# Two heads in one kernel (a long convolution and linear attention): constants in another order, head masks made late, the ones column carried by x, due times per stage

## The chip, the cores and the metric

The kernel runs on one core of a Trainium2 chip. The core has five engines, each with its own queue of instructions that it takes in order: PE (TensorE, matrix products into PSUM), DVE (VectorE), ACT (ScalarE), POOL (GpSimd) and SP (SyncE, which here only issues DMAs). They run side by side and wait for each other through semaphores. The metric is the device time of one execution in microseconds (us). PSUM has eight banks of 128 x 512 float32; PE can't write a bank until its last reader is done with it.

## The reference

The output is 2048 x 1152 in bfloat16: the left 576 columns come from part A, the right 576 from part B.

```python
# A: k shifted over four taps, times v, a convolution over the sequence, times q
k_shift = sum over t of k_pad[:, t:t + S, :] * shift_k[:, ks - 1 - t]
kv = k_shift * v
y = irfft(rfft(kv, 2S) * rfft(ssm_k, 2S))[:S] + kv * ssm_D
a = q * y
# B: linear attention with 32 heads of 18 features
q, k, v = split(x @ wqkv)
phi = lambda t: where(t > 0, t + 1, exp(t)) + 1e-6
kv  = phi(k)^T v   (per head);   z = sum over s of phi(k)
o   = (phi(q) kv) / (phi(q) z + 1e-6)
b   = o @ wo
```

S is 2048 and D is 576 in both.

## The kernel before

Both parts run interleaved, so that one has work for an engine where the other waits. Nothing of the order is written out by hand: each step is given to a planner (`_Sched`) as an operation with a due time (`key`), an assumed duration for each engine that could do it, the operations it depends on and the buffers it uses. `plan()` then plays the program through: of all operations that could go it takes the one that could start first, ties by due time. Evictions of PSUM may go to ACT or DVE (`evac`, `copy`, L337 to L343); the planner takes the engine on which they would end first, with `PEN` added for DVE. Evictions are made due `EVK` earlier. The planned order becomes the program order of each engine; on the chip only semaphores set the times.

**Constants** (`_consts_fft`, L76 to L137; `_consts_b`; `_consts_heads`, L42 to L73) are made ahead of the planned program. The Fourier matrices Gre and Gim (128 x 16 x 128) are sines of integers that DVE works out (L92 to L97) from iotas of POOL; the small matrix Wsm is a sine too (L136). ACT needs another function table for sines than for exponentials and loads it with a separate instruction. `_consts_heads` makes the masks that cut the products of heads out of larger products (maskbd with fourteen selects of 18 columns, L47 and L49), selectors and ones. They are read by the stages kv, z, bc of part B.

**Part B.** x is loaded in four DMAs (L369), transposed on PE in eight groups (L387) and copied to xT (L341 or L339). Its last tile holds features 448 to 575 in rows 0 to 127, of which row 0 is overwritten with ones by a memset on POOL (L394), and the weights have a row of ones at the same place (L324), which adds one to each product. K is 16 row blocks in two halves of 288 columns, each of five matmuls (L408); ACT takes the exponential (phi_k, L411), DVE makes phi (pk, L414). G is x^T phi(k) (L438), with a column of ones behind x and behind pk (L420, L421) that gives the sums; then the small stages kv, z, M; then four groups of q (L552, L555, L560), denominators (L572 to L585), their transposes and spreading to features (L605), the products (L611), and the output product (L629), evicted to ob and stored (L635).

**Part A** runs in five chunks of channels, four of 128 and one of 64 (`chunk`, from L685). For each: load of the filter (h_sb, L697), transposing load of k (kT, L700), loads of v and q for pairs of chunks (L670), the diagonal matrices of the taps (dg, L709, on DVE), transposes of the filter (hT, L721), a first Fourier step s1 (L739, evicted to Ch or Cu), a transpose of 32 x 32 blocks on DVE (L755), a second step s2 with Wsm (L770, evicted to Th or Tu), a copy X of Th with rows exchanged by DMA (L791), the taps (cv, L806) and u = taps times v (L813). Then the products of the spectra (L825), the way back: is1 (L841), its eviction V, a transpose Vt (L853), is2 (L866, L867), the product with q (L873) and the store (L878).

All DMAs go through SP's queue. Dc and swT (L647 to L653) are tiny loads of ssm_D and shift_k; Ere and Eim are Gre and Gim transposed by DMA. The due times of part A are linear in the stage: `k0(t)` is the start of the chunk plus t times one factor.

Of the kernel before, what the change touches and what calls it, by code (L numbers as in the profile page):

```python
# [20 lines left out]
FX = [0, 128, 256, 384, 448]  # L21
# [7 lines left out]
EVK, HK = 2.75, 1.0  # L29
TB0, TBS = 8.0, 1.44  # L30
TA0, TAP = 12.0, 24.83
# [10 lines left out]
def _consts_heads(nc, cpool, K):  # L42
    maskbd = cpool.tile([128, 126], FP32, name="maskbd")
    nc.gpsimd.memset(maskbd[:], 1.0)
    for hh in range(7):
        blk = maskbd[:, hh * 18:(hh + 1) * 18]
        nc.gpsimd.affine_select(out=blk, in_=blk, compare_op=ALU.is_ge, fill=0.0, base=-18 * hh,  # L47
                                pattern=[[0, 18]], channel_multiplier=1)
        nc.gpsimd.affine_select(out=blk, in_=blk, compare_op=ALU.is_ge, fill=0.0, base=18 * hh + 17,  # L49
                                pattern=[[0, 18]], channel_multiplier=-1)  # L50
# [25 lines left out]
def _consts_fft(nc, cpool, cw, K):  # L76
# [29 lines left out]
    def field(name, shift, mask):  # L106
        t = tmp.tile([128, 1], I32, name=name + "_i")
        if shift:
            nc.vector.tensor_single_scalar(out=t[:], in_=pidx[:], scalar=shift, op=ALU.logical_shift_right)
        nc.vector.tensor_single_scalar(out=t[:], in_=t[:] if shift else pidx[:], scalar=mask, op=ALU.bitwise_and)  # L110
        f = tmp.tile([128, 1], FP32, name=name)
        nc.vector.tensor_copy(out=f[:], in_=t[:])
        return f
    lo4, b4 = field("lo4", 0, 15), field("b4", 4, 1)
    hi4, b0 = field("hi4", 1, 15), field("b0", 0, 1)
# [6 lines left out]
    for w, (row, ri, coef, ipat, base, opat) in enumerate(spec):  # L122
# [5 lines left out]
        if ri is not None:  # L128
            oc = tmp.tile([128, 1], FP32, name="oc%d" % w)
            nc.vector.tensor_scalar(out=oc[:], in0=ri[:], scalar1=coef, scalar2=None, op0=ALU.mult)  # L130
            nc.vector.tensor_scalar(out=off[:, w, :], in0=off[:, w, :], scalar1=oc[:, 0:1], scalar2=None, op0=ALU.add)
        nc.vector.scalar_tensor_tensor(out=wi[:, w, :], in0=idx[:, w, :], scalar=row[:, 0:1], in1=off[:, w, :],
# [16 lines left out]
class _Op:  # L149
    def __init__(self, key, eng, fn, deps, bufs, dma):  # L150

        if any(x.cls == 'PS' for x in bufs) and 'PE' not in eng:
            key -= EVK
# [3 lines left out]
        self.start = self.end = None  # L157
        for b in bufs:
            b.users.append(self)


class _Sched:
# [3 lines left out]
    PEN = 0.23  # L166
# [8 lines left out]
    def op(self, key, eng, fn, deps=(), bufs=(), dma=0.0):  # L175
        o = _Op(key, eng, fn, list(deps), list(bufs), dma)
        self.ops.append(o)
        return o
# [21 lines left out]
    def plan(self):  # L200
        left = list(self.ops)
        order = []
        while left:
            best = None
            for o in left:
                if any(d.end is None for d in o.deps):
                    continue
                ready, taken, ok = 0.0, {}, True
# [23 lines left out]
                rank = (round(st, 2), o.key)  # L232
                if best is None or rank < best[0]:
                    best = (rank, fin, e, st, o, taken)
            if best is None:
                raise RuntimeError("no operation can go: %s" % [o.key for o in left[:8]])
# [11 lines left out]
            left.remove(o)  # L248
            order.append(o)
        order.sort(key=lambda o: o.start)  # L250
# [12 lines left out]
def kernel(  # L263
# [30 lines left out]
                 {'PE': 6.0, 'ACT': 9.5, 'DVE': 9.0, 'POOL': 8.0, 'SP': 0.8})  # L294
# [14 lines left out]
    K = {}  # L309
    cwork = [work.tile([128, 4096], BF, name="cw%d" % i, tag="W8_%d" % i) for i in range(2)]  # L310
    _consts_fft(nc, cpool, cwork, K)
# [5 lines left out]
    nc.gpsimd.memset(neg1[:], -1.0)  # L317
    Ere = cpool.tile([128, 16, 128], BF, name="Ere")
    Eim = cpool.tile([128, 16, 128], BF, name="Eim")
    xT = cpool.tile([128, 5, S], BF, name="xT")  # L320
    wk = cpool.tile([128, 5, D], BF, name="w_k")
    for w in (wk,):
        nc.gpsimd.memset(w[0:64, 4, :], 0.0)
        nc.gpsimd.memset(w[0:1, 4, :], 1.0)  # L324
    _consts_heads(nc, cpool, K)
# [8 lines left out]
    for t in rb:  # L334
        nc.gpsimd.memset(t[:], 0.0)
# [9 lines left out]
    def evac(n):  # L345
        return {'ACT': 0.2 + n * 0.0008, 'DVE': 0.07 + n * 0.00104}
# [6 lines left out]
    tB = [TB0]  # L353

    def kb(cost):
        tB[0] += cost * TBS
        return tB[0] - cost * TBS

    xb = _Buf('X18', 'x_sb')
    pb = _Buf('X18', 'pk')  # L360

    def xview(b):
        return b.t.rearrange("p (r f) -> p r f", f=D + 1)

    xv = x.rearrange("(r p) f -> p r f", p=128)
    d_x, o_xT = [], []

    def load_x(g):
        d_x.append(dma(0.1 if g == 0 else 1.5 + 0.1 * g, 0.59, lambda g=g: nc.sync.dma_start(  # L369
            out=xview(xb)[:, 4 * g:4 * g + 4, 0:D], in_=xv[:, 4 * g:4 * g + 4, :]), (), (xb,)))  # L370

    load_x(0)
    d_w = [dma(1.0, 0.59, lambda: nc.sync.dma_start(
        out=wk[:, 0:4, :], in_=wqkv[0:512, D:2 * D].rearrange("(t p) n -> p t n", p=128)))]
    d_w.append(dma(1.1, 0.08, lambda: nc.sync.dma_start(out=wk[64:128, 4, :], in_=wqkv[512:576, D:2 * D])))
    for g in range(1, 4):
        load_x(g)

    for g in range(8):
        key = TB0 + g * 2.4 * TBS - 1.5  # L380
        ps = _Buf('PS', 'xT_ps', 2)

        def mm(e, g=g, ps=ps):
            pv = ps.t.bitcast(BF)[:, 0:1280].rearrange("p (t s) -> p t s", t=5)
            for rr in range(2):
                for t in range(5):
                    nc.tensor.transpose(out=pv[:, t, 128 * rr:128 * (rr + 1)],  # L387
                                        in_=xview(xb)[:, 2 * g + rr, FX[t]:FX[t] + 128], identity=ident[:])
        o1 = op(key, {'PE': 0.58}, mm, [d_x[g // 2]], (ps, xb))

        def f(e, g=g, ps=ps):
            copy(e, xT[:, :, 256 * g:256 * (g + 1)],
                 ps.t.bitcast(BF)[:, 0:1280].rearrange("p (t s) -> p t s", t=5))
            nc.gpsimd.memset(xT[0:1, 4, 256 * g:256 * (g + 1)], 1.0)  # L394
# [521 lines left out]
```

## Time and profile before

| | |
|---|---|
| median of 3 runs | 200.14 us (199.23 to 200.71) |
| the profiled execution | 199.92 us |
| its span (first to last instruction) | 198.2 us |
| PE busy | 171.6 us, 87% |
| DVE busy | 174.9 us, 88% |
| ACT busy | 126.5 us, 64% |
| POOL busy | 15.8 us, 8% |
| DMA traffic | 25.81 MB |
| mean granted clock of PE | 0.971 |

A group of the profile gives line, engine, operation, output and inputs by the program's names, how often it ran, its busy time, the mean time of one, and the idle time of its engine just before it with the engine that ended it. A line of the order of time gives start and length, then the same names; a bracket at its end is idle time of that engine before it. A row of stretches gives for each engine the busy time within these microseconds. In the line of slices each digit is a fortieth of the span, in tenths.

### The profile page before, as it was taken

The page shows a single profiled execution, that of the slowest core. Times are in us where ns is not written, and L with a number is a line of the kernel's source. Part 1 is how long each engine was busy: PE and PEld are TensorE (multiplying, and loading weights), DVE is VectorE, ACT ScalarE, POOL GpSimd, SP SyncE. Part 2 cuts the span into 40 slices and gives each one's busy share as a digit, 9 for nine tenths or more (in the row PEclk, how much of TensorE's full clock was granted, in tenths as well). Part 3 has the DMA queues.
Part 4 walks back from the last instruction along what each step waited for, and adds up shares of the span by engine and source line. Part 5 has one row for each costly group of instructions (what it writes and reads, how often), then busy time and mean ns, then how long its engine had stood idle before and what let it go on. Part 6 is the DMA issues. An engine that isn't in the chain of part 4 may idle for free. (4 is left out here: it accounts for less than half of the span.)

```text
span 198.2 us, 5391 instructions
## 1 busy us (share of the span) xinstructions
PE 171.6 (87%) x2277; PEld 130.2 (66%) x2277; DVE 174.9 (88%) x259; ACT 126.5 (64%) x176; POOL 15.8 (8%) x60
## 2 busy tenths in 40 slices
PE   0449999989999999999999999799986999869660
PEld 0426888977688788778577677676765786427450
DVE  7943588999997997899999899999999999999880
ACT  3566878289576755775558978337982749760440
POOL 8970100001000000010000000000000000000000
PEclk9999999999999999999999999999999999985995
DMA  5999999321293049029703934150410130212733
GB/s 188 351 327 227 184 215 313 85 107 47 80 254 82 0 167 256 7 58 312 117 0 113 310 59 146 55 139 0 88 60 33 72 143 13 80 49 90 208 123 55
DMA packets 43548, 25.81 MB, mean 130 GB/s; under 512 B 23044, under 2 KB 41732, under 8 KB 43524
## 3 DMA queue, kind: packets, MB, share of 16 engines
q1 hardware_dynamic: 43524, 25.47, 47.8%
q8 instruction: 17, 0.28, 0.6%
q14 instruction: 7, 0.06, 0.1%
HBM read 12.36 MB, written 4.72 MB: 86 GB/s over the span
## 5 line engine op out<-in xcount | busy, mean ns | idle before, releaser
L408 PE MATMUL ps_all<-w_k,xT 128*128 128x288 bf16 x160 | 24.4, 313 | 4.6 <-DVE xT L341 2.2
L552 PE MATMUL ps_all<-xT,w_k 128*126 128x512 bf16 (+1 forms) x100 | 24.2, 381 | 1.8 <-DVE late_q L611 1.6
L629 PE MATMUL ps_all<-late_w,late_q 126*128 126x288 bf16 (+1 forms) x160 | 23.0, 288 | 1.6 <-DVE late_q L611 1.6
L408 PEld LDWEIGHTS <-xT 128*128 128x128 bf16 x160 | 16.5, 106 | 10.9 <-POOL xT L394 2.6
L806 PEld LDWEIGHTS <-kT 128*128 128x128 bf16 x320 | 21.0, 151 | 2.3 <-issue 1.6
L438 PE MATMUL ps_all<-pk,x_sb 128*128 128x288 bf16 (+1 forms) x160 | 22.2, 287 | 0.0
L806 PE MATMUL ps_all<-dg,kT 128*128 128x128 bf16 (+1 forms) x320 | 21.6, 226 | 0.7 <-DVE Tu L341 0.5
L555 ACT ACTIVATE phi_q<-ps_all,neg_133 126x512 bf16<-126x512 f32 (+1 forms) x20 | 13.6, 687 | 12.8 <-PE ps_all L552 9.2
L414 DVE SCALAR_TENSOR_TENSOR pk<-phi_k,ps_all 128x288 bf16<-128x288 bf16 x32 | 13.5, 449 | 8.1 <-ACT phi_k L411 7.9
L339 ACT ACTIVATE Th<-ps_all 128x1024 bf16<-128x1024 f32 x14 | 13.8, 1021 | 9.2 <-PE ps_all L770 9.1
L411 ACT ACTIVATE phi_k<-ps_all,neg_133 128x288 bf16<-128x288 f32 x32 | 15.5, 501 | 5.8 <-PE ps_all L408 4.4
L629 PEld LDWEIGHTS <-late_q 126*128 126x128 bf16 (+1 forms) x160 | 14.8, 98 | 6.7 <-DVE late_q L611 1.9
L339 ACT ACTIVATE Tu<-ps_all 128x1024 bf16<-128x1024 f32 x11 | 11.0, 1022 | 11.3 <-PE ps_all L770 11.2
L853 DVE STREAM_TRANSPOSE Vt<-V 128x1024 f32<-128x1024 f32 x9 | 18.0, 1995 | 0.2
L438 PEld LDWEIGHTS <-x_sb 128*128 128x128 bf16 x160 | 14.8, 98 | 4.8 <-issue 1.4
L552 PEld LDWEIGHTS <-w_k 128*126 128x126 bf16 (+1 forms) x100 | 12.3, 131 | 8.6 <-issue 2.2
L339 ACT ACTIVATE ob<-ps_all 128x288 bf16<-128x288 f32 x29 | 11.4, 410 | 8.6 <-PE ps_all L629 8.4
L339 ACT ACTIVATE Ch<-ps_all 128x1024 bf16<-128x1024 f32 (+1 forms) x15 | 14.4, 988 | 2.6 <-PE ps_all L739 2.6
L339 ACT ACTIVATE Cu<-ps_all 128x1024 bf16<-128x1024 f32 (+1 forms) x16 | 14.5, 950 | 1.0 <-PE ps_all L739 0.8
L339 ACT ACTIVATE V<-ps_all 128x1024 bf16<-128x1024 f32 x14 | 13.8, 1021 | 1.8 <-PE ps_all L841 1.7
L611 DVE SCALAR_TENSOR_TENSOR late_q<-late_q,ps_all 126x512 bf16<-126x512 bf16 (+1 forms) x20 | 12.4, 679 | 0.6 <-PE ps_all L605 0.6
L560 DVE SCALAR_TENSOR_TENSOR late_q<-phi_q,ps_all 126x512 bf16<-126x512 bf16 (+1 forms) x20 | 12.9, 669 | 0.0
(129 smaller groups left out, 316.0 us busy)
## 6 DMA issues: line engine op xcount, KB each, us to landing
X<-Th SPq DMA_DIRECT2D x18, 256.0 KB, 2.3
h_sb<-in_A_ssm_k_dram SPq DMA_DIRECT2D x5, 512.0 KB, 5.4
x_sb<-in_B_x_dram SPq DMA_DIRECT2D x4, 576.0 KB, 5.0
out_dram<-ob SPq DMA_DIRECT2D x16, 144.0 KB, 1.7
v_p<-in_A_v_dram SPq DMA_DIRECT2D x2, 1024.0 KB, 9.3
q_p<-in_A_q_dram SPq DMA_DIRECT2D x2, 1024.0 KB, 6.5
out_dram<-q_p SPq DMA_DIRECT2D x2, 1024.0 KB
w_k<-in_B_wqkv_dram SPq DMA_DIRECT2D x2, 576.0 KB, 4.4
```

Source lines behind the costliest of these rows:

```text
L339: nc.scalar.activation(out=out_ap, in_=in_ap, func=ACT.Copy, scale=scale)
L408: nc.tensor.matmul(ps.t[:, 0:n1 - n0], lhsT=xT[:, t, r * 128:(r + 1) * 128], rhs=wk[:, t, n0:n1], start=(t == 0), stop=(t == 4))
L411: o2 = op(key, {'ACT': 0.46}, lambda e, ps=ps, eb=eb: nc.scalar.activation(out=eb.t[:, 0:288], in_=ps.t[:, 0:288], func=ACT.Exp, bias=neg1 ...
L414: nc.vector.scalar_tensor_tensor(out=xview(pb)[:, r, n0:n1], in0=eb.t[:, 0:288], scalar=1.0, in1=ps.t[:, 0:288], op0=ALU.min, op1=ALU.max),
L438: nc.tensor.matmul(ps.t[:, 0:n1 - n0], lhsT=xview(xb)[:, r, f0:f0 + 128], rhs=xview(pb)[:, r, n0:n1], start=(r == 0), stop=(r == 15))
L552: nc.tensor.matmul(ps.t[0:hn, 512 * j:512 * (j + 1)], lhsT=wq[:, t, h0:h0 + hn], rhs=xT[:, t, 512 * g:512 * (g + 1)], start=(t == 0), stop ...
L555: o2 = op(key, {'ACT': 0.2 + 0.4 * n}, lambda e, ps=ps, eb=eb, hn=hn, n=n: nc.scalar.activation(out=eb.t[0:hn, 0:512 * n], in_=ps.t[0:hn, ...
L560: nc.vector.scalar_tensor_tensor(out=pqT(g)[0:hn, c:c + n, :], in0=eb.t[0:hn, 0:512 * n].rearrange("p (c n) -> p c n", n=512), scalar=1.0, ...
L611: nc.vector.scalar_tensor_tensor(out=o, in0=o, scalar=EPS, in1=ps.t[0:hn, 0:512 * n].rearrange("p (c n) -> p c n", n=512), op0=ALU.add, op ...
L629: nc.tensor.matmul(ps.t[:, 0:288], lhsT=pqT(g)[0:hn, c, rr * 128:(rr + 1) * 128], rhs=wview(2)[0:hn, c, n0:n1], start=(c == 0), stop=(c == 4))
L806: nc.tensor.matmul(pv[:, bi, 0:dc], lhsT=kTb.t[:, c0:c0 + 16 * 127 + 1:16], rhs=dg[:, j, 0:dc], start=(j == 0), stop=(j == 3))
L853: nc.vector.transpose(out=vt[:, 32 * c:32 * (c + 1), :], in_=V.t[:, 2048 * c:2048 * (c + 1)].bitcast(FP32).rearrange("p (w r) -> p w r", r ...
```

## The change

It does the following:

- The ones column of x is written once by DVE, before x is loaded, and the last tile of xT takes columns 449 to 576 of x instead of 448 to 575, so that row 127 is the column of ones. The weights have their row of ones at 127; the memsets of xT are gone. Two memsets of w_k stand ahead of all other constants on POOL.
- The head masks and two zeroed tiles become one planned operation on POOL (`o_late`), on which the stages that read them depend; maskbd is made by two selects instead of fourteen.
- dg is made by POOL instead of DVE.
- The small fields of the index arithmetic are made by five operations instead of ten; the reciprocal writes bfloat16 itself.
- x's first quarter is loaded in two halves, with the weights between them.
- The assumed durations, the start of each engine, `PEN`, `EVK` and all due times are other numbers; each stage of a chunk has its own due time, and each part of B its own pace.
- The planner's search is written with counters, and ties go by the number of the operation.

In the built program PE has as many matmuls as before. Other instructions change engine by the plan. DVE has 2 more evictions of xT, 1 of V, 3 of ob, 1 of late_q, and fewer of Tu (7 to 2), Cu (4 to 2), Ch (5 to 3), hT, Th, GT (5 to 3), late_w; ACT has the counterparts, and four loads of its function table instead of two. In SP's queue the first chunk's h_sb stands behind x, the weights and the four tiny loads; kT's loads stand between the two pairs of X.

```diff
-FX = [0, 128, 256, 384, 448]
-EVK, HK = 2.75, 1.0
-TB0, TBS = 8.0, 1.44
-TA0, TAP = 12.0, 24.83
+P_B0 = 8.00
...
+P_T0 = 19.57
+P_T1 = 37.72
+P_T2 = 63.63
+P_T3 = 84.60
+P_T4 = 111.14
+P_SC = 0.81
+P_h = -15.98
+P_k = -15.51
...
+P_x = -16.80
+P_cv = 10.00
...
+P_p0 = 26.46
+P_p1 = 55.86
...
+P_EVK = 2.69
+P_PEN = 0.43
...
-    maskbd = cpool.tile([128, 126], FP32, name="maskbd")
+    maskbd = cpool.tile([128, 7, 18], FP32, name="maskbd")
     nc.gpsimd.memset(maskbd[:], 1.0)
-    for hh in range(7):
-        blk = maskbd[:, hh * 18:(hh + 1) * 18]
-        nc.gpsimd.affine_select(out=blk, in_=blk, compare_op=ALU.is_ge, fill=0.0, base=-18 * hh,
-                                pattern=[[0, 18]], channel_multiplier=1)
...
+    nc.gpsimd.affine_select(out=maskbd[:], in_=maskbd[:], compare_op=ALU.is_ge, fill=0.0, base=0,
+                            pattern=[[-18, 7], [0, 18]], channel_multiplier=1)
+    nc.gpsimd.affine_select(out=maskbd[:], in_=maskbd[:], compare_op=ALU.is_ge, fill=0.0, base=17,
+                            pattern=[[18, 7], [0, 18]], channel_multiplier=-1)
...
+    for i, (shift, mask) in enumerate(((0, 15), (4, 1), (1, 15), (0, 1))):
+        nc.vector.tensor_scalar(out=fi[:, i:i + 1], in0=pidx[:], scalar1=shift, scalar2=mask,
+                                op0=ALU.logical_shift_right, op1=ALU.bitwise_and)
+    nc.vector.tensor_copy(out=ff[:], in_=fi[:])
...
-                rank = (round(st, 2), o.key)
+                rank = (round(st, 2), o.key, o.num)
...
-                 {'PE': 6.0, 'ACT': 9.5, 'DVE': 9.0, 'POOL': 8.0, 'SP': 0.8})
+                 {'PE': 5.0, 'ACT': 10.3, 'DVE': 8.5, 'POOL': 6.5, 'SP': 1.2})
...
+    nc.vector.memset(xview(xb)[:, :, D:D + 1], 1.0)
     cwork = [work.tile([128, 4096], BF, name="cw%d" % i, tag="W8_%d" % i) for i in range(2)]
+    wk = cpool.tile([128, 5, D], BF, name="w_k")
+    nc.gpsimd.memset(wk[96:128, 4, :], 1.0)
+    nc.gpsimd.memset(wk[0:64, 4, :], 0.0)
     _consts_fft(nc, cpool, cwork, K)
...
+    nc.gpsimd.memset(xview(pb)[:, :, D:D + 1], 1.0)
...
-    for w in (wk,):
-        nc.gpsimd.memset(w[0:64, 4, :], 0.0)
-        nc.gpsimd.memset(w[0:1, 4, :], 1.0)
-    _consts_heads(nc, cpool, K)
...
+    def late_consts(e):
+        _consts_heads(nc, cpool, K)
+        for t in rb:
+            nc.gpsimd.memset(t[:], 0.0)
+    o_late = op(12.0, {'POOL': 7.0}, late_consts)
...
-        return {'ACT': 0.2 + n * 0.0008, 'DVE': 0.07 + n * 0.00104}
+        return {'ACT': 0.2 + n * 0.0008, 'DVE': 0.14 + n * 0.00105}
...
-    def kb(cost):
-        tB[0] += cost * TBS
-        return tB[0] - cost * TBS
+    def kb(cost, pace):
+        tB[0] += cost * pace
+        return tB[0] - cost * pace
...
+    load_x(0.1, 0, 2)
+    d_w = [dma(0.2, 0.08, lambda: nc.sync.dma_start(out=wk[63:127, 4, :], in_=wqkv[512:576, D:2 * D]), rate=340.0),
+           dma(0.3, 0.59, lambda: nc.sync.dma_start(
+               out=wk[:, 0:4, :], in_=wqkv[0:512, D:2 * D].rearrange("(t p) n -> p t n", p=128)), rate=340.0)]
+    load_x(0.4, 2, 4)
     for g in range(1, 4):
-        load_x(g)
+        load_x(1.5 + 0.1 * g, 4 * g, 4 * g + 4)
...
-                                        in_=xview(xb)[:, 2 * g + rr, FX[t]:FX[t] + 128], identity=ident[:])
+                                        in_=xview(xb)[:, 2 * g + rr, FT[t]:FT[t] + 128], identity=ident[:])
...
-            nc.gpsimd.memset(xT[0:1, 4, 256 * g:256 * (g + 1)], 1.0)
...
-    o_kv = op(key, {'DVE': 1.0}, f, [o1], (ps,))
+    o_kv = op(key, {'DVE': 1.3}, f, [o1, o_late], (ps,))
...
-            nc.vector.reciprocal(out=rden, in_=den)
-            nc.vector.tensor_copy(out=rb[g % 2][:, :, 0:32], in_=rden.rearrange("p (r h) -> p r h", h=32))
+            with nc.allow_low_precision(reason="operand of TensorE"):
+                nc.vector.reciprocal(out=rb[g % 2][:, :, 0:32], in_=den.rearrange("p (r h) -> p r h", h=32))
...
-        T = TA0 + sum(ACH[c][1] for c in ORDER[:n]) / 128.0 * TAP
-        k0 = lambda t: T + t * f * TAP / 30.0 * 1.01
+        T = (P_T0, P_T1, P_T2, P_T3, P_T4)[n]
+        k0 = lambda t: T + t * f * P_SC
...
-                nc.vector.tensor_scalar(out=dg[:, j, 0:dc], in0=ident[:, lo:lo + dc],
+                nc.gpsimd.tensor_scalar(out=dg[:, j, 0:dc], in0=ident[:, lo:lo + dc],
                                         scalar1=swf[:, ci, j:j + 1], scalar2=None, op0=ALU.mult)
-        o_dg = op(k0(-5), {'DVE': 0.5}, fn, [o_sw, g1.get('cv')], (dgb,))
+        o_dg = op(k0(P_dg), {'POOL': 1.3}, fn, [o_sw, g1.get('cv')], (dgb,))
```

## The prediction

> **What bounds the kernel now.** I read the page's busy shares and slices first, then the order of time at the start, then a table of stretches at the end, then the groups by shape.
>
> ```profile
> PE 171.6 (87%) x2277; PEld 130.2 (66%) x2277; DVE 174.9 (88%) x259; ACT 126.5 (64%) x176; POOL 15.8 (8%) x60
> PE   0449999989999999999999999799986999869660
> DVE  7943588999997997899999899999999999999880
> ```
>
> PE and DVE are both near full from slice 4 to slice 36; ACT has a third of the span free and POOL nearly all of it. So two things cost time: what keeps PE from starting, and where DVE is so full that PE waits for it. The start:
>
> ```profile
> 9.94 0.81 DVE L341 COPY xT<-ps_all 128x1280 bf16<-128x1280 bf16 x1
> 10.81 1.14 PE L408 MATMUL ps_all<-w_k,xT 128*128 128x288 bf16 x4 [2.20 <-DVE xT L341]
> 13.50 0.17 POOL L420 MEMSET x_sb<- 128x16 bf16 x1 [0.46 <-DMA x_sb<-in_B_x_dram]
> 13.60 0.60 POOL L394 MEMSET xT<- 1x256 bf16 x2
> 14.00 6.64 PE L408 MATMUL ps_all<-w_k,xT 128*128 128x288 bf16 x31 [2.05 <-POOL xT L394]
> 22.77 5.68 PE L408 MATMUL ps_all<-w_k,xT 128*128 128x288 bf16 x45
> ```
>
> Four of the five matmuls of the first K group run at 10.81; the fifth needs the row of ones in xT's last tile. That memset stands in POOL's queue behind the head masks and behind the ones columns of x, which wait for x to land. K runs only from 14.00. Its first 31 matmuls take 6.64/31 = 0.214 us each, later ones 5.68/45 = 0.126. The end:
>
> ```profile
> 165.00:170.00 5.00, 5.00 (x89) 3.56 (x92) 4.91 (x7) 3.98 (x8) 0.00 (x0) 1.00 0.10 32
> 170.00:175.00 5.00, 4.02 (x94) 1.97 (x95) 4.93 (x6) 4.47 (x7) 0.00 (x0) 1.00 0.25 89
> 175.00:180.00 5.00, 3.44 (x19) 2.04 (x20) 4.89 (x6) 1.94 (x2) 0.00 (x0) 0.65 0.28 108
> 180.00:185.00 5.00, 3.66 (x41) 2.50 (x39) 4.75 (x6) 1.02 (x1) 0.00 (x0) 0.67 0.05 14
> ```
>
> (Columns: PE, PEld, DVE, ACT, POOL busy; granted clock; DMA share; GB/s.) From 170 on DVE is full and PE is not; PE's clock falls to two thirds as well. From DVE's eviction of Tu at 162.20 to its end at 192.8 DVE has 30.5 us of work in 30.6 us. The last 20 us belong to DVE, and from 20 to 160 PE idles only 5.4 us (stretches of 20 us), 3.5 of it from 120 to 160, where DVE is at 19.7 of 20.
>
> **The change, part by part.** The sum stands against the profiled execution: span 198.2, its own time 199.92, so 1.7 lie around the span; the median of the runs shown, 200.14, is 0.2 more.
>
> *Ones carried by x.* The eight memsets of xT (L394) go; row 127 of w_k's last tile holds ones and x's own column of ones is transposed along. K's fifth matmul then waits only for the xT copy and the weights. When does that copy come? Two memsets of w_k (0.57 us for 64 rows in the trace; I take about 1.1 for both) now stand before the iotas on POOL, so DVE's chain of table arguments, 1.27 to 8.47 before, starts near 2.4 and ends near 9.6. In the built order the first xT copy follows right behind four tiny operations, so it ends near 10.7: K starts at 10.7 as its first four matmuls did, but isn't stopped. Gross gain 14.00 - 10.7 = 3.3 us, plus the third x transpose, moved ahead of K.
>
> *Two more table loads.* In the built order ACT runs Sin, Exp once, Sin again for Wsm, then Exp: four loads instead of two, 1.28 each by the row at L411. Last Gre ends about 12.4 (11.2 before plus the 1.1 of shift), load to 13.7, phi_k 14.2, load 15.5, Wsm 15.9, load 17.1. So the second phi_k starts near 17.1, where before the first started at 15.80. What covers it: PE is slow then (0.214 per matmul, 1.1 us per half row block), and from 10.7 it has four K groups, one x transpose and three more K groups in line, about 7 us, before it needs banks that phi_k frees. From 17.1 ACT gives one phi_k per 0.52 and starts the eighth at 20.2, where before, with PE slow and three transposes of x between, the eighth started at 22.37. So of the 3.3 some 1.1 is lost: net gain of the start 2.2.
>
> Here the Trainium skill speaks against the change ("ScalarE: Activation LUTs", "What ACT_TABLE_LOAD costs"): a switch of tables costs the load of about 1283 ns and a drain of some 1380 ns, 2.66 us in all. In the trace the load at L411 starts at 14.51 and the first phi_k at 15.80: 1.29, with no drain to be seen, though ACT had been idle just before. By the page phi_k would be dense only from 19.9 (two more drains, 2.8), and the start would lose 0.6 instead of gaining 2.2. I take the row; both ends stay in the range.
>
> *DVE relieved.* From the built orders, counted against the rows by shape:
>
> ```profile
> L341 DVE CAST Tu<-ps_all 128x1024 bf16<-128x1024 f32 x7 | 8.5, 1210 | 0.0
> L339 ACT ACTIVATE Tu<-ps_all 128x1024 bf16<-128x1024 f32 x11 | 11.0, 1022 | 11.3 <-PE ps_all L770 11.2
> L709 DVE TENSOR_SCALAR dg<-ident,swf 128x128 bf16<-128x128 bf16 x16 | 2.8, 241 | 0.1
> L132 DVE SCALAR_TENSOR_TENSOR wi<-idx,hi_101,off 128x32 int32<-128x32 f32 x2 | 1.3, 628 | 0.0
> L132 DVE SCALAR_TENSOR_TENSOR wi<-idx,lo_91,off 128x32 int32<-128x32 f32 x1 | 0.2, 234 | 0.0
> L61 POOL TENSOR_SCALAR_AFFINE_SELECT esel<-esel 128x630 bf16<-128x630 bf16 x1 | 0.7, 734 | 0.0
> ```
>
> DVE loses 5 Tu (6.05), 2 Cu (2.44), 2 Ch (1.90), one hT (1.22), one Th (1.21), 2 GT (1.03), one late_w (0.74), all dg (3.5), the casts of the reciprocal (4 x 0.23 = 0.9) and a few field operations (0.3): 19.3. It gains 2 xT (1.63), one V (1.22), 3 ob (1.32), one late_q (0.39), a small memset (0.1): 4.7. Net -14.6 of 174.9. ACT gains 5 Tu, 2 Cu, 2 Ch, hT, Th, 2 GT, one late_w and two loads (16.1), loses 2 xT, one V, 3 ob, one late_q (5.3): +10.7, to 137 of 198. PE has the same 2277 matmuls. The reciprocal writing bf16 itself lies between 0.95 (its own row, near) and one cast more; I take 0.95. What it is worth: up to 160 only PE's 5.4 us of idle time, 3.5 of it under a full DVE; I take 3.0.
>
> *dg on POOL.* The trace has no such operation there. Nearest rows: memset of 128x128 0.20, affine_select 0.73 for 630 elements; so 0.2 to 0.85 each, 4 to 17 us over 20, on an engine with 180 us free, and dg is built a whole chunk ahead of its matmuls. Against it speaks the skill ("SBUF — State Buffer", "SBUF: two separate sides"): DVE operations with two SBUF inputs and GpSimd operations that read SBUF exclude each other for a whole instruction. The rows show it: L132 with two SBUF inputs takes 628 ns beside POOL's 734 ns select, 234 without. By that rule the worst is 20 x 0.85 = 17 us of DVE time; but the operations of that kind that recur, the products of L825, are 22 us of the span, 11%, so some two of twenty collide: under 1 us, taken from DVE's new slack. I take 0. Below nothing it cannot come beyond the 3.5 already counted.
>
> *Masks late.* Fourteen selects become two (0.2 to 0.85 each); they end near 11, and their first readers stand behind all of K and G. 0. *DMA queue.* h_sb of the first chunk goes from first place to behind x, the weights and four small loads. The first small one held SP from 6.85 to 13.1 with 4.6 MB ahead; with 3.0 MB ahead I estimate it free near 10, h_sb issued near 12.5, landed by 18 (5.4 to landing); its transposes come after 50 K matmuls, near 21. 0, at worst 2. kT's transposes (5 to 6 us of issue) now stand between the two X pairs of a chunk; between the s2 stage that feeds the second pair and the u stage that its product also needs lie at least 9 us of PE work in every chunk (matmuls in the built order by the rows' time). 0.
>
> *The end.* In the built order DVE's work from the Tu eviction of the same stage to its last product, by the same rows, is 27.1 us (30.5 before). That Tu comes after 2 us more PE work. So it starts at 162.2 + 2.0 - 2.2 - 3.0 = 159.0; 27.1 of work and some 1.9 of waiting for PE and for two V evictions now both on ACT (2.0 in a row where before DVE took one) give 188.0; then, as before, 5.4 for the last store (192.8 to 198.2). The 1 MB store now leaves some 5 us before the last one instead of 10; at 6.5 to landing it is covered, 1 us if not. Span 193.4, time **195.1**.
>
> **Rivals.** *More:* the early start is kept whole (1.1), the remaining 2.4 us of PE's idle time shrink by two thirds (1.6), and PE's clock isn't lowered at the end (the 32 matmuls of is2 from 178.6 to 182.0 took 3.4 us; 16 transposes of that width at 144.8 took 1.16, so some 2.3 at full clock: 1.1): 191.3. Against it: before that is2 PE still waits for DVE's transpose of V. *Half:* the start's gain is eaten by table loads and banks, or PE stays the bound in the middle: only one of 2.2 and 3.0 comes: 198.1 or 197.3, and up to 200.5 where the end keeps its length too. I put it at 198.1. *Slower:* ACT becomes the engine that frees the banks. It carries 10.7 us more, all in order, and PE can't pass a bank it waits for; in 20 to 60 ACT is already busy 30.0 of 40 us. If half of the 10.7 stands before PE and DVE's relief of 3.0 is not used: 195.1 + 5.3 + 3.0 = 203.4. It decides from about 7 us of PE waiting for ACT (5.0 of gain in the forecast, and 2 to be seen as slower); in the waits of before, the largest such entry is 0.6 us. Against it: ACT's longest idle times are waits for PE.
>
> **How the numbers follow.** Forecast 0.52 (193 to 198), more 0.18 (190 to 193), half 0.18 (197 to 200.5, a third of it under 198.1), slower 0.12. About 1% is what a measurement of this kernel can tell from no change (198.1 to 202.1). Faster 0.52 + 0.18 + 0.06 = 0.76, same 0.12, slower 0.12. The range 190 to 200.5 leaves out slower and a little of more.
>
> **What would show it.** K running without a gap from about 10.7; no wait of PE for POOL; four table loads with phi_k dense from about 17; DVE near 160 us busy, ACT near 137; the DVE-full stretch at the end some 3.5 us shorter. I am wrong if PE's waits for ACT exceed 7 us, if the first h_sb comes late, if DVE's operations stretch beside dg on POOL, or if the last store queues behind the large one.

## The result and the profile after

| | before | after |
|---|---|---|
| median of the runs side by side | 199.69 us (198.57 to 200.71) | 191.89 us (190.70 to 193.42, 4 runs) |
| the profiled execution | 199.92 us | 191.29 us |
| its span | 198.2 us | 189.6 us |
| PE, DVE, ACT, POOL busy | 171.6, 174.9, 126.5, 15.8 us | 166.2, 160.6, 133.7, 23.3 us |

The ratio is 0.9615 with a 95% interval of 0.9522 to 0.9709: 7.7 us of 200. All ratios here compare undisturbed executions alone, so one can differ from the ratio of two medians (it does in e3 below, whose ratio rests on two of six executions, 194.70 and 196.98; the other four took 197.89 to 200.08).

The busy shares and four of the lines of slices of the page after (PEclk is the granted clock of PE, in tenths):

```profile
PE 166.2 (88%) x2277; PEld 129.7 (68%) x2277; DVE 160.6 (85%) x224; ACT 133.7 (71%) x185; POOL 23.3 (12%) x59
...
PE   0593999999999999989999999999999899979630
...
DVE  5974769877498898999999999799998998999960
ACT  2599389568698446669966979787977947978500
...
PEclk9998799999999999999999999999999999999965
```

DVE has 14.3 us less than before and ACT 7.2 more, though ACT didn't become a bound. PE has fewer gaps, but a deep one in slice 4 (14.2 to 19.0 us) that the kernel before had not, and its clock is lowered from the end of that slice into slice 5. The order of time on PE at the start:

```profile
9.47 1.25 PE L439 MATMUL ps_all<-ident,x_sb 128*128 128x128 bf16 x10 [0.43 <-DMA x_sb<-in_B_x_dram]
10.51 2.89 PE L459 MATMUL ps_all<-w_k,xT 128*128 128x288 bf16 x20
13.24 0.72 PE L439 MATMUL ps_all<-ident,x_sb 128*128 128x128 bf16 x10
13.80 2.00 PE L459 MATMUL ps_all<-w_k,xT 128*128 128x288 bf16 x15
18.69 1.23 PE L439 MATMUL ps_all<-ident,x_sb 128*128 128x128 bf16 x10 [2.89 <-DVE xT L396]
19.71 2.78 PE L459 MATMUL ps_all<-w_k,xT 128*128 128x288 bf16 x15
22.33 1.16 PE L766 MATMUL ps_all<-ident,h_sb 128*128 128x128 bf16 x16
```

K runs from 10.51 without a wait for POOL, and in this execution at once at 0.145 us per matmul. At 15.80 PE runs out of work and waits 2.89 us for a copy of xT. The ten transposes behind that wait take 1.23 us where the ten ahead of it took 0.72, and fifteen K matmuls take 2.78 instead of 2.00. The first filter's transposes (L766) still come at 22.33, before at 28.28. The largest waits of PE:

```profile
PE ps_all L439 <- POOL ident L72: 5.0, 1, 5.0
PE ps_all L912 <- DVE Vt L899: 4.0, 1, 4.0
PE ps_all L439 <- DVE xT L396: 2.9, 1, 2.9
PE ps_all L439 <- DMA x_sb<-in_B_x_dram: 2.0, 2, 1.6
PE ps_all L851 <- ACT Ch L394: 0.7, 1, 0.7
```

The first, third and fourth lie ahead of 20 us and the second in the last 12 us; nothing between is over 0.7, and the largest for ACT is 0.7. The table of stretches at the end (columns as before):

```profile
160.00:165.00 5.00, 4.94 (x84) 2.97 (x82) 4.96 (x8) 4.80 (x9) 0.00 (x0) 1.00 0.18 62
165.00:170.00 5.00, 3.43 (x44) 1.53 (x43) 5.00 (x7) 3.69 (x7) 0.00 (x0) 1.00 0.17 59
170.00:175.00 5.00, 5.00 (x80) 3.59 (x67) 4.66 (x6) 4.59 (x8) 0.00 (x0) 1.00 0.40 148
175.00:180.00 5.00, 3.35 (x72) 2.83 (x71) 5.00 (x5) 2.57 (x5) 0.00 (x0) 1.00 0.22 78
180.00:185.00 5.00, 1.86 (x32) 1.70 (x31) 3.38 (x4) 0.38 (x1) 0.00 (x0) 0.67 0.70 213
```

DVE is still full in the tail, but the clock stays at 1.00 until 180; before, it was 0.65 and 0.67 from 175 to 185.

### The profile page after: what moved, and what is told of

Read it like the earlier page. It is cut to its first block, busy times and chain, and to the rows that moved or that the text cites. A ratio compares the mean times of both kernels' runs of the same rounds, so it can differ in the third digit from the quotient of the medians.

```text
span 189.6 us, 5361 instructions
## 1 busy us (share of the span) xinstructions
PE 166.2 (88%) x2277; PEld 129.7 (68%) x2277; DVE 160.6 (85%) x224; ACT 133.7 (71%) x185; POOL 23.3 (12%) x59
## 4 chain that ended last, share of the span: by engine, by line
PE 78%; ACT 8%; DVE 4%; DMA 3%; issue 2%; POOL 1%; SPq 1%; ACTq 1%; DVEq 0%; POOLq 0%
PE ps_all L597 11%; PE ps_all L483 11%; PE ps_all L851 11%; PE ps_all L674 9%; PE ps_all L459 9%; PE ps_all L784 8%; PE ps_all L815 3%; DMA x_sb<-in_B_x_dram 3%; PE ps_all L766 3%; PE ps_all L887 2%; PE ps_all L912 2%; PE ps_all L439 2%; PE ps_all L913 2%; PE ps_all L650 1%; ACT L462 1%
## 5 line engine op out<-in xcount | busy, mean ns | idle before, releaser
L459 PE MATMUL ps_all<-w_k,xT 128*128 128x288 bf16 x160 | 22.6, 295 | 0.0
L851 PEld LDWEIGHTS <-kT 128*128 128x128 bf16 x320 | 21.3, 151 | 1.6 <-issue 1.0
L394 ACT ACTIVATE Th<-ps_all 128x1024 bf16<-128x1024 f32 x15 | 14.7, 1022 | 9.4 <-PE ps_all L815 9.4
L394 ACT ACTIVATE Tu<-ps_all 128x1024 bf16<-128x1024 f32 x16 | 15.6, 1023 | 6.4 <-PE ps_all L815 6.3
L394 ACT ACTIVATE Cu<-ps_all 128x1024 bf16<-128x1024 f32 (+1 forms) x18 | 16.7, 982 | 4.6 <-PE ps_all L784 4.6
L483 PEld LDWEIGHTS <-x_sb 128*128 128x128 bf16 x160 | 14.9, 98 | 5.0 <-issue 1.5
L462 ACT ACTIVATE phi_k<-ps_all,neg 128x288 bf16<-128x288 f32 x32 | 14.1, 509 | 4.8 <-PE ps_all L459 4.6
L439 PE MATMUL ps_all<-ident,x_sb 128*128 128x128 bf16 x80 | 7.8, 264 | 9.9 <-POOL ident L72 5.0
L394 ACT ACTIVATE Ch<-ps_all 128x1024 bf16<-128x1024 f32 (+1 forms) x17 | 15.6, 964 | 1.2 <-PE ps_all L784 1.1
L394 ACT ACTIVATE V<-ps_all 128x1024 bf16<-128x1024 f32 x13 | 12.9, 1025 | 5.0 <-PE ps_all L887 4.9
L600 ACT ACTIVATE phi_q<-ps_all,neg 126x512 bf16<-126x512 f32 (+1 forms) x20 | 13.5, 688 | 2.4 <-PE ps_all L597 1.5
L439 PEld LDWEIGHTS <-x_sb 128*128 128x128 bf16 x80 | 6.6, 120 | 10.7 <-DMA x_sb<-in_B_x_dram 6.4
```

The source lines that it names most:

```text
L394: nc.scalar.activation(out=out_ap, in_=in_ap, func=ACT.Copy, scale=scale)
L439: nc.tensor.transpose(out=pv[:, t, 128 * rr:128 * (rr + 1)], in_=xview(xb)[:, 2 * g + rr, FT[t]:FT[t] + 128], identity=ident[:])
L459: nc.tensor.matmul(ps.t[:, 0:n1 - n0], lhsT=xT[:, t, r * 128:(r + 1) * 128], rhs=wk[:, t, n0:n1], start=(t == 0), stop=(t == 4))
L462: o2 = op(key, {'ACT': 0.5}, lambda e, ps=ps, eb=eb: nc.scalar.activation(out=eb.t[:, 0:288], in_=ps.t[:, 0:288], func=ACT.Exp, bias=neg1[ ...
L483: nc.tensor.matmul(ps.t[:, 0:n1 - n0], lhsT=xview(xb)[:, r, f0:f0 + 128], rhs=xview(pb)[:, r, n0:n1], start=(r == 0), stop=(r == 15))
L600: o2 = op(key, {'ACT': 0.21 + 0.48 * n}, lambda e, ps=ps, eb=eb, hn=hn, n=n: nc.scalar.activation(out=eb.t[0:hn, 0:512 * n], in_=ps.t[0:hn ...
```

## The experiments

Eleven kernels, each against the kernel before on the same chip. "The changed kernel" is the one after, with its plan kept where only an instruction is swapped. Differences in us follow from ratios times 200. The change's own interval, from four runs, is 1.9 us to each side; a smaller difference from it isn't told by the ratios.

| | edit | ratio, 95% interval |
|---|---|---|
| | the change | 0.9615, 0.9522 to 0.9709 |
| e1 | dg back on DVE | 0.9605, 0.9573 to 0.9637 |
| e2 | ones of xT by POOL again | 0.9625, 0.9592 to 0.9657 |
| e3 | six Tu evictions back on DVE | 0.9792, 0.9737 to 0.9848 |
| e4 | Wsm's sine ahead of the first exponential | 0.9446, 0.9415 to 0.9478 |
| e5 | before, with the ones carried by x | 0.9872, 0.9844 to 0.9900 |
| e6 | old due times, new assumed durations | 1.0225, 1.0200 to 1.0250 |
| e7 | new due times, old assumed durations | 1.0124, 1.0090 to 1.0158 |
| e8 | e4 with the ones by POOL | 0.9497, 0.9461 to 0.9533 |
| e9 | all old numbers, new instructions | 0.9914, 0.9898 to 0.9930 |
| e10 | old offsets of A's stages only | 0.9989, 0.9963 to 1.0016 |
| e11 | one factor 0.81 to 0.83 | 1.0043, 1.0022 to 1.0064 |

### The start: e5, e2, e4, e8

e5 puts the first part of the change alone into the kernel before; the planner plans anew.

```diff
+    nc.vector.memset(xview(xb)[:, :, D:D + 1], 1.0)
...
-                                        in_=xview(xb)[:, 2 * g + rr, FX[t]:FX[t] + 128], identity=ident[:])
+                                        in_=xview(xb)[:, 2 * g + rr, FT[t]:FT[t] + 128], identity=ident[:])
...
-            nc.gpsimd.memset(xT[0:1, 4, 256 * g:256 * (g + 1)], 1.0)
```

> The kernel before with one part of the change alone: x carries its ones column (written by DVE ahead of x's loads), so the eight POOL memsets of xT go; plan, masks, table loads and evictions stay as before. If POOL's queue is what holds K until 14.0: K runs from 10.8 without a stop, 2 to 3 us faster than before. If the start is absorbed by what is full later (DVE from 160 on): less than 1 us faster.

Measured: median 197.44, 2.6 us gained. DVE's load is as before (174.5 busy), its evictions are the same in number, and the tail has its lowered clock (0.76 from 180 on, as before): the start's gain comes through to the end.

e2 takes the same part out of the changed kernel.

```diff
-                                        in_=xview(xb)[:, 2 * g + rr, FT[t]:FT[t] + 128], identity=ident[:])
+                                        in_=xview(xb)[:, 2 * g + rr, FX[t]:FX[t] + 128], identity=ident[:])
...
+            nc.gpsimd.memset(xT[0:1, 4, 256 * g:256 * (g + 1)], 1.0)
```

> The changed kernel with the plan kept, only the row of ones of xT written by POOL memsets again (old column window of x, old row of the weights). POOL is busy with constants until 12.4 in the changed kernel, so K's fifth matmul should wait from 10.7 to about 12.7, and the fifth xT group behind dg until about 20.7. If the start counts in full: 2 us slower than the changed kernel. If what is lost at the start is hidden by the stall that PE has anyway at 15.8 to 18.7: under 1 us.

Measured: median 192.83, and a ratio within the interval of the change. In the changed kernel the ones by x are worth nothing that can be told here. The reason is in the profile: PE's 2.9 us wait for xT is gone from the waits of e2. K is stopped again after four matmuls, from about 11.9 to 12.58, and its next sixteen are slow (4.02 us); that fills the gap, and the first filter's transposes come at 22.52 instead of 22.33. Two delays stand one behind the other, and the first takes its time out of the second.

e4 removes the second delay. The bias of phi_k is made from Wsm, so that the sine of Wsm must come ahead of the first exponential, and ACT loads two tables instead of four.

```diff
-    nc.gpsimd.memset(neg1[:], -1.0)
+    nc.vector.tensor_scalar(out=neg1[:], in0=W[:, 0, 0:1], scalar1=0.0, scalar2=-1.0, op0=ALU.mult, op1=ALU.add)
```

> The changed kernel, only the bias of the exponential is made by DVE from Wsm (times 0, minus 1), so that Wsm's sine comes before the first exponential and two of the four table loads go. Phi_k should run densely from about 15.0 instead of 16.4. If the two loads cause PE's wait of 2.9 us at 15.8 to 18.7 (the fourth xT copy stands behind pk in DVE's queue): that wait falls to about 1.5 and the slow matmuls after it become fast, 1 to 2 us faster than the changed kernel. If the time is set further on: within 0.5 us.

Measured: median 188.63 (188.00 to 189.89), 3.4 us faster than the change and 11.1 faster than before: the best of all kernels. ACT's order of time in the changed kernel:

```profile
11.65 1.28 ACT L462 ACT_TABLE_LOAD   x1 [0.27 <-PE ps_all L459]
12.95 0.50 ACT L462 ACTIVATE phi_k<-ps_all,neg 128x288 bf16<-128x288 f32 x1
13.46 1.28 ACT L167 ACT_TABLE_LOAD   x1
14.76 0.37 ACT L167 ACTIVATE Wsm<-wi,negpi 128x96 bf16<-128x96 int32 x1
15.15 1.28 ACT L462 ACT_TABLE_LOAD   x1
```

and in e4:

```profile
12.64 0.37 ACT L167 ACTIVATE Wsm<-wi,negpi 128x96 bf16<-128x96 int32 x1 [1.25 <-DVE wi L165]
13.28 1.28 ACT L462 ACT_TABLE_LOAD   x1 [0.27 <-DVE neg L372]
14.57 2.85 ACT L462 ACTIVATE phi_k<-ps_all,neg 128x288 bf16<-128x288 f32 x7
```

phi_k is dense from 14.57 instead of 16.44. Why 1.9 us there make 3.4 at the end is to be seen on DVE, in the changed kernel:

```profile
13.48 0.46 DVE L465 SCALAR_TENSOR_TENSOR pk<-phi_k,ps_all 128x288 bf16<-128x288 bf16 x1 [0.88 <-ACT phi_k L462]
16.98 0.85 DVE L465 SCALAR_TENSOR_TENSOR pk<-phi_k,ps_all 128x288 bf16<-128x288 bf16 x2 [3.04 <-ACT phi_k L462]
17.74 0.17 DVE L699 CAST swf<-swT 128x20 f32<-128x20 bf16 x1
17.82 0.82 DVE L396 COPY xT<-ps_all 128x1280 bf16<-128x1280 bf16 x1
```

DVE is idle for 3.04 us at a pk that waits for the second phi_k, and the fourth xT copy stands behind it in DVE's queue. PE waits for that copy, and then works at half its clock. The stretches of the changed kernel around that wait:

```profile
16.00:18.00 2.00, 0.00 (x0) 0.00 (x0) 1.02 (x4) 1.99 (x6) 0.00 (x0) 0.97 0.83 180
18.00:20.00 2.00, 1.31 (x12) 1.22 (x12) 1.84 (x6) 0.90 (x3) 1.99 (x4) 0.50 1.15 346
20.00:22.00 2.00, 2.00 (x13) 1.36 (x12) 1.46 (x3) 0.58 (x2) 0.36 (x1) 0.68 1.15 345
```

and the same of e4, where PE waits only 0.4 us for that copy:

```profile
16.00:18.00 2.00, 1.60 (x19) 1.25 (x18) 2.00 (x6) 1.43 (x4) 1.47 (x3) 1.00 0.83 178
18.00:20.00 2.00, 2.00 (x22) 1.69 (x20) 2.00 (x6) 1.20 (x3) 0.89 (x2) 1.00 1.15 346
20.00:22.00 2.00, 2.00 (x30) 1.84 (x28) 1.84 (x3) 0.95 (x2) 1.18 (x3) 1.00 1.15 342
```

The granted clock (third column from the right) is the difference: 2.5 us less of waiting, and some 1.3 less of slow work (1.23 + 2.78 against 0.72 + 2.00). Against that, e4's first twenty K matmuls took 1.1 us more (3.98 against 2.89), so that the first filter's transposes come at 19.60, 2.7 us earlier than in the change; the other 0.6 comes in the tail. Part of the 2.7 is the execution: in e3, which starts with the same instructions as the change and loads four tables, the twenty took 4.16, PE waited 1.98 us, its clock stayed at 1.00, and the filter's transposes came at 21.35, 1.8 us behind e4.

e8 is e4 with the ones by POOL, the memset of e2.

> The version with a single table switch (188.6 us), with the row of ones of xT written by POOL again. If the POOL memset cost only 0.9 us before because the stall by the table loads hid it, it shows now: K waits from 10.4 to about 12.5 and the time is 1.5 to 2.5 us above 188.6. If the wait is worth little by itself: under 1 us.

Measured: median 189.78, about 1.0 us slower than e4, with intervals that just overlap. With the gap gone, the ones by x may be worth about 1 us; this isn't certain. The profiled execution of e8, its fastest, doesn't show it: K waits from 12.0 to 12.57, but its next sixteen matmuls take only 2.46 us, and the span is e4's, 186.3.

### DVE's relief: e1, e3

e1:

```diff
-                nc.gpsimd.tensor_scalar(out=dg[:, j, 0:dc], in0=ident[:, lo:lo + dc],
+                nc.vector.tensor_scalar(out=dg[:, j, 0:dc], in0=ident[:, lo:lo + dc],
```

> The changed kernel with the plan kept as it is, only dg made by DVE again at the same places of the order (20 operations, some 3.5 us of DVE time). If DVE's relief counts where DVE is full, little of this counts, since the five dg stand in the first two thirds of the run where DVE is now 76 to 95% busy: 0 to 1.5 us slower than the changed kernel. If every us of DVE time counts: 3.5 us slower. If dg on POOL stands in DVE's way through shared access to SBUF: faster by up to 1 us.

Measured: median 192.23, no difference that can be told. DVE is 2.6 us busier (163.2), but PE idles as little from 20 to 160 as in the change (2.4 and 2.5 us), and the span is 190.1, 0.5 more. The 3.5 us of "every us counts" are ruled out; zero and 1 us aren't told apart. The two groups of the changed kernel that the step was about:

```profile
L754 POOL TENSOR_SCALAR dg<-ident,swf 128x128 bf16<-128x128 bf16 x16 | 9.4, 605 | 5.6 <-DVE swf L699 5.6
L871 DVE TENSOR_TENSOR Th<-Tu,Th 128x2048 bf16<-128x2048 bf16 x9 | 10.9, 1210 | 0.3 <-ACT Tu L394 0.2
```

605 ns on POOL lie within the bounds taken (200 to 850). The products of spectra, with two inputs in SBUF, take 1210 ns as before (1221), but that says nothing of the lock that the prediction weighed: the five blocks of dg run at 18.0, 23.6, 51.2, 80.3 and 112.7 (for 1.7 to 2.4 us each), and no product runs within them; the nearest start at 54.88 and 83.96. No run here tests it.

e3 moves six of Tu's evictions back to DVE, in the same places of the order:

```diff
+TU = ((0, 1, 1), (1, 0, 1), (1, 1, 1), (2, 0, 1), (2, 1, 1), (3, 1, 1))
...
+                        if which == 'u' and (n, c, ip) in TU:
+                            e = 'DVE'
```

> The changed kernel with the plan kept, but six evictions of Tu, one for each half chunk but one, moved from ACT back to DVE at their places in the order: DVE +7.3 us, ACT -6.1 us, so DVE near 168 us. If the balance of evictions is what freed PE in the middle and at the end: 3 us slower (2 to 5). If it doesn't matter and the due times did it: within 1 us.

Measured: 3.5 us slower than the change by the ratios, 7.0 by the medians (198.89); the profiled execution, the fastest of the six, has a span of 193.0, 3.4 more, although its start is 1.0 us ahead of the change's (21.35 against 22.33). Six evictions of 1.21 us are 7.3 us of DVE's time, so they cost at least half of themselves. PE idles 4.5 us from 20 to 160 instead of 2.5, and the largest new wait says how (L651 in e3 is L650 of the change, the spreading of the denominators to features):

```profile
PE ps_all L651 <- DVE Tu L397: 1.4, 1, 1.4
```

A Tu eviction frees a bank that PE waits for. dg frees nothing: it is ready a chunk ahead. That this is why the one costs and the other doesn't is read from these waits; equal sums of DVE time were not moved.

### The plan: e9, e7, e6, e10, e11

e9 keeps every edit of the instructions and gives the planner all old numbers: due times, assumed durations, starts, PEN and EVK (the new parameters allow it, since the old ones are linear).

> All edits of the instructions kept (ones by x, masks late, dg on POOL, fields, reciprocal, order of the loads), with the old assumed durations, starts, PEN and EVK and the old due times. Theory (the start is worth 2.5 us as in the kernel before with the ones alone, dg and the casts of the reciprocal take 4.4 us off DVE, and the plan's numbers are the rest): 194 to 197 us. Rival 1 (the edits of the instructions are nearly all of the gain): 191 to 193 us. Rival 2 (they need the new numbers): 198.5 to 202 us.

Measured: median 198.59, 1.7 us gained; the theory of 194 to 197 fell, and the second rival came, at its edge. The instructions alone bring less than a quarter of the gain, and the numbers 6.0 us. e9 loads four tables too, so what the instructions gain at its start is partly lost there.

e7 and e6 take half of the numbers back: the assumed durations (`PEN` 0.23, evictions on DVE 0.07 + n 0.00104, Vt 1.15 instead of 2.0, and the like), and the due times.

```diff
-P_T0 = 19.57
+P_T0 = 12.0
...
-P_s1u = 17.96
+P_s1u = 14
...
-P_p1 = 55.86
+P_p1 = 25
```

> The changed kernel planned with the old assumed costs (evictions on DVE 0.07 + 0.00104 n, penalty of DVE 0.23, transposes and products 1.15, the eviction times of K and q); new due times and all other edits stay. Its plan has about 15.7 us more evictions on DVE than the changed kernel, so DVE near 176 busy as before, and four table loads. If the balance of evictions set the time: 198 to 203. If the due times carry the gain: within 2 us of the changed kernel, 190 to 194.

> The changed kernel planned with the old due times (linear in the stage, one pace for part B, the old EVK); new costs and all other edits stay. Its plan has 8.4 us more evictions on DVE than the changed kernel and only two table loads. If the balance of evictions and the table loads set the time: + about 6 for DVE by the run with six Tu moved, - about 3 for the loads, so 193 to 197. If the due times by themselves (which chunk runs when) carry the gain: 198 or more.

Measured: 202.42 and 204.26, both slower than the kernel before. Each fell in the range that was to say that the half taken back carries the gain. Both can't carry it: each half of the new numbers is worse without the other than the old numbers together (e9). e10 takes back only the offsets of A's stages, so that they are linear again, with the chunks' starts and B's paces new.

> The changed kernel with the old linear offsets of part A's stages; the chunks' starts, the paces of part B and all assumed durations stay new. Theory (due times and assumed durations only work together, and what the plan must get right is the order of the stages within a chunk): 198 to 204 us, as with all due times old. Rival (chunk starts and paces are what matters, offsets of stages are details): 191 to 194 us.

Measured: median 200.41, as slow as before. e11 changes one number:

```diff
-P_SC = 0.81
+P_SC = 0.83
```

> The changed kernel with one due-time factor changed from 0.81 to 0.83, which gives another plan throughout (Tu on DVE 5 instead of 2, ob 2 instead of 6, V 3 instead of 5). Theory (the plan's quality is a matter of some microseconds, and a small step away from the numbers given costs part of it): 193 to 197 us. Rival (the numbers stand for a broad range, any near plan is as good): 191 to 192.8 us. Second rival (the numbers given are one lucky point, near plans lose all the gain): 198 us and more.

Measured: median 201.24 (199.36 to 202.26, 12 runs). The whole gain is lost, although DVE is busy for 162.5 us only, 1.9 more than in the change (in its profiled execution, the slowest of the twelve). The expectation that a near plan loses a part fell; the second rival is what came. The table takes the start of the last u product of the last chunk (L813 before, L858 after, L861 in e3) as a mark in each profiled execution:

| | DVE busy | last u product | from there to the end |
|---|---|---|---|
| before | 174.9 | 161.6 | 36.6 |
| the change | 160.6 | 157.2 | 32.4 |
| e4 | 160.3 | 154.5 | 31.8 |
| e3 | 166.7 | 159.9 | 33.1 |
| e9 | 170.7 | 163.3 | 33.6 |
| e10 | 168.0 | 161.5 | 37.4 |
| e11 | 162.5 | 162.2 | 38.3 |
| e7 | 174.0 | 158.7 | 41.1 |
| e6 | 170.0 | 163.3 | 39.2 |

DVE's busy time doesn't put these plans in order. Against the change, e10, e11 and e6 lose about as much ahead of the mark (4.3, 5.0 and 6.1 us) as in the tail (5.0, 5.9 and 6.8); e7 loses 8.7 of its 10.2 in the tail. Of e11's 5.0, the start makes 1.3 (the first filter's transposes come at 23.64 instead of 22.33) and PE's idle time from 20 to 160 another 1.3 (3.8 us instead of 2.5); the rest wasn't followed. In e11 PE's order of time in the tail:

```profile
174.19 0.65 PE L815 MATMUL ps_all<-Cth,Wsm 32*32 32x512 bf16 x13 [2.53 <-DVE late_q L656]
174.77 2.83 PE L674 MATMUL ps_all<-late_w,late_q 126*128 126x288 bf16 x10
```

DVE's at the same place:

```profile
171.13 0.68 DVE L656 SCALAR_TENSOR_TENSOR late_q<-late_q,ps_all 126x512 bf16<-126x512 bf16 x1
171.72 1.89 DVE L899 STREAM_TRANSPOSE Vt<-V 128x1024 f32<-128x1024 f32 x1
173.48 2.44 DVE L656 SCALAR_TENSOR_TENSOR late_q<-late_q,ps_all 126x512 bf16<-126x512 bf16 x4
```

and in the change:

```profile
165.44 1.28 DVE L656 SCALAR_TENSOR_TENSOR late_q<-late_q,ps_all 126x512 bf16<-126x512 bf16 x2
166.63 1.92 DVE L899 STREAM_TRANSPOSE Vt<-V 128x1024 f32<-128x1024 f32 x1
168.42 1.84 DVE L656 SCALAR_TENSOR_TENSOR late_q<-late_q,ps_all 126x512 bf16<-126x512 bf16 x3
```

In e11 one product of late_q stands ahead of the Vt transpose, in the change two. PE wants the bank that the second frees, and waits 2.53 us; in the change its longest wait there is 0.63. Then the clock falls (the stretches of e11):

```profile
172.00:174.00 2.00, 0.00 (x0) 0.00 (x0) 2.00 (x2) 0.00 (x0) 0.00 (x0) 0.85 0.08 27
174.00:176.00 2.00, 1.75 (x18) 0.55 (x18) 2.00 (x5) 1.09 (x2) 0.00 (x0) 0.50 0.00 0
176.00:178.00 2.00, 2.00 (x22) 0.85 (x22) 2.00 (x2) 1.51 (x3) 0.00 (x0) 0.50 0.00 0
```

and ten output products take 2.83 us; ten of them took 1.41 in the change:

```profile
170.06 1.41 PE L674 MATMUL ps_all<-late_w,late_q 126*128 126x288 bf16 x10
```

The next twenty take 3.64, where two tens at the change's rate are 2.8. So the wait costs its 2.5 us and about as much again. This is the largest piece of e11's tail that its profile shows; the order wasn't mended on its own, so that this swap makes the 5.9 us of tail isn't shown. Nor was it tried which of the new numbers does the most.

## Why the prediction was right, and where its sizes were off

The direction was right, and the time within the range: 195.1 with 190.0 to 200.5 against 191.89. Of the mechanism, the earlier start, DVE's relief and the shorter tail are all there. But the prediction added up what the built orders give each engine to do. Such a sum would have forecast a gain for e11 as well, where DVE has 12.4 us less than before and all of the gain is lost. That the sums came out is therefore in part luck: what makes this order a good one isn't in them. The time came out at the number of the rival "more" (191.3), and one of its three reasons holds as it was meant, the clock in the tail.

| | forecast | measured |
|---|---|---|
| DVE's eviction of Tu in the last chunk starts | 159.0 | 157.77 |
| from it to DVE's end | 29.0 | 27.2 (to 184.97) |
| from there to the last store's end | 5.4 | 4.6 |
| span | 193.4 | 189.6 |

- *Ones by x, K's start.* K isn't stopped and doesn't wait for POOL, as forecast. That it starts at 10.51 where 10.7 was said is luck: the first xT copy, forecast to end near 10.7, ends at 9.69 (8.88 plus 0.81), and K stands behind the third x transpose, which waits 0.43 us for x to land and runs from 9.47. The net gain of the start was mis-sized: 2.2 forecast; by difference (4.4 earlier at the tail, plus the 2.0 of work that was moved ahead, less 2.9 of idle time of PE) it is 3.5. The term that was left out is the slow matmuls: 31 at 0.214 us instead of 0.126 cost the kernel before 2.7 us, and in this execution they are not slow. Of that not all is the change's doing: with much the same first instructions, 20 K matmuls took 2.89 us here and 4.16, 3.98, 3.68 and 3.55 in e3, e4, e10 and e11. The rival "more" had the early start kept whole (1.1); the size came, but by these fast matmuls and not because the table loads were harmless.
- *Two more table loads.* This step failed: 1.1 forecast, 3.4 measured in e4. Taking the row for the loads and no drain was right: the load at 11.65 ends at 12.93, and the exponential starts at 12.95. The 2.66 us that the Trainium skill ("ScalarE: Activation LUTs", "What ACT_TABLE_LOAD costs") has for a switch with its drain would, by estimate, have put it at 14.3. The forecast covered the loads with 7 us of PE work, counted at the slow rate; it was done in 5.3 us. And it asked only for banks: what was late was the fourth xT copy, behind a pk on DVE.
- *DVE relieved.* Worth of 3.0 for 14.6 us: PE's idle time from 20 to 160 went from 5.4 to 2.5, so the figure held. The way to it doesn't: e1 shows nothing that can be told for dg, e3 at least a half for Tu, and in e9, with 4.2 us of relief, that idle time is 8.2. e11 shows that a relief of 12.4 us (174.9 to 162.5) may bring nothing in all. DVE's relief was 14.3 us, near the 14.6; ACT's share was mis-sized, 10.7 more forecast and 7.2 measured.
- *dg on POOL, masks late, the DMA queue.* 0, 0 and 0: e1 shows nothing against the first; PE has no wait for a mask or for the first h_sb among its largest. The masks and the DMA order were not run alone. The row of L132 that was read as 234 ns without a select beside it isn't clean: it runs at 10.67, beside the last of L49's short selects (9.73 to 10.87).
- *The end.* Two errors. The rows of DVE's work were added up (27.1) and 1.9 of waiting put on top. But rows of DVE that follow each other overlap by about 0.1 us here (the u product at 157.16 takes 0.69, and Tu starts at 157.77): DVE's busy time in the tail is 25.1 us, and with 2.1 of waiting the tail takes 27.2. In the kernel before the same rows add to 30.5, while DVE is busy for 29.1 of 31.2. And DVE's end of before was read as 192.8, the end of the first of its last two products; it is 193.43, so that the last store took 4.8 and not 5.4.
- *The clock.* That it isn't lowered in the tail was a term of the rival "more" (1.1), and it came: 1.00 until 180, and the 32 matmuls of is2 run from 175.8 to 177.8 where they took 3.4 us before. The rival's other reason, that the last 2.4 us of PE's idle time shrink, did not: 2.5 are left.
- *Slower by ACT.* Did not come: ACT has 7.2 us more, and PE's waits for it make 3.0 us in all, none over 0.7.

## What to carry to other kernels

Judge a plan by its queues, not by its sums. Here a step that frees a bank was worth half its time or more when it moved, one that is ready early nothing that could be measured, and one number of the planner nudged by 2.5% lost the whole gain of 7.7 us. When two delays end close together, taking one away shows little until the other goes as well, so test each edit with the other delay removed. Look for what changes a function table in the start-up and put it ahead of the first use of the other table.

## What the runs showed of the hardware

- A wait of PE of 2.5 to 2.9 us costs more than itself. In the change the granted clock falls to 0.50 some 2.1 us after PE's wait began at 15.80 (0.97 over 16 to 18), and is back near 21.3 (0.68 over 20 to 22), 2.6 us after PE went on. In e11 it falls 1.7 us into the wait and is back at about 180.2, 6.0 us after. The wait of 1.98 us in e3 and others of 0.4 to 0.7 us left it at 1.00. But one long wait isn't needed: in the kernel before, the clock fell near 176.5, where the longest wait ahead of it was 0.96 us and PE had been busy for 2.6 of the 4.5 us from 172.0. The Trainium skill ("TensorE: Matmul & The Clock Gate", "Part 1: The HAM clock gate") has the half rate come after an idle window of about 3.4 us, by windows that run freely; here shorter waits were enough, and what share of busy time keeps the clock up no run here tells.
- POOL makes a product of 128x128 bfloat16 with a scalar per partition in 605 ns, and one of 128x64 in 443 ns; DVE took 241 for the first in the kernel before.
- The recorded clock doesn't show PE's slow start. In the kernel before, 31 matmuls of K from 14.00 took 0.214 us each, and in e4 twenty from 10.43 took 0.199, both in stretches whose granted clock reads 1.00.
